# Attention and two mixtures of experts on one core: plain first layers accumulated in three PSUM banks, a fourth id table, lists ahead of weights

## The chip, the cores and the metric

The kernel runs on 1 core of a Trainium2 chip. The metric is the device time of one execution in microseconds (us); the number given for a kernel is the median of its runs. The kernel before takes 1922.17 us (three runs, 1922.14 to 1926.21).

## The reference

In float32: linear attention with exponential features over 4 batches, 8 heads, 576 positions and head size 64; its result, reshaped to 2304 tokens of 512 features, goes through a first mixture of 8 experts that uses every expert with weights balanced by 8 rounds of row and column scaling, and then through a second mixture that sends each token to one expert.

```python
# first mixture
P = np.exp(logits)
for _ in range(8):
    P /= P.sum(1, keepdims=True) + 1e-09
    P /= P.sum(0, keepdims=True) + 1e-09
    P *= N / E
for e in range(E):
    h = np.maximum(x @ w1[e], 0.0)      # 512 -> 1024
    out += P[:, e:e + 1] * (h @ w2[e])  # 1024 -> 512
# second mixture
logits = xn @ en.T / tau                # xn, en: normalised rows
expert_idx = np.argmax(logits, axis=1)
for e in range(E):
    h = np.maximum(x[mask] @ w1[e], 0.0)
    out[mask] = gate_w[mask, None] * (h @ w2[e])
```

## The kernel before

Every float32 operand is split in a high and a low part, so that one product of 128x128 by 128x384 is two contraction steps of three matmuls, six in all (`product`, L407, matmuls at L410 to L412).

The first mixture is cut in 16 groups n (8 experts, each with two halves of its hidden layer) and 3 blocks of 768 tokens. One group on one block is a half h, so h runs from 0 to 47; the program walks `HS` in that order. A two-by-two Strassen-like scheme replaces 8 products by 7. In groups 1 to 14 the second layer of one half is interleaved with the first layer of the next (`layers`, L465). Groups 0 (h = 0, 1, 2) and 15 (h = 45, 46, 47) are plain: `p1_group` (L564) makes the hidden layer in 14 products, seven for each j (a half of the hidden columns): A11, S2, S3, S1, A12, A22, S4, named by their weights; `p2_plain` then makes 16 products, which DVE adds to the accumulators at L833. h=0 is interleaved with the end of attention, since its generator `first` is created there and a piece is taken after each stage of the attention pipeline.

A finished quarter of the hidden layer goes through `put`: for n=0 `plain` (L417: ACT relu, then DVE's low part), for n=15 `gated`, where `gate` (L426) on DVE multiplies the relu with the token's weight into `graw` or in the bank; then ACT casts the high part (L432 or L442) and POOL (L443) or DVE (L433) subtracts for the low part. Each yield of a generator is a tick; a step is attached to tick k of half h by a table.

Routing for the second mixture: logits (`route_l`, `route_a`, L880), then small DVE work on the counts, which yields `meta` (offset, expert, and whether its weights have to be loaded, per block of 128 slots) and for each tile of 128 tokens the slots `si`. `route_i` (L951) on POOL scatters token number and gate of one tile into one of RB id tables in DRAM; a scatter that reuses a table waits for the earlier one on it. A block's list is the sum of the RB tables: `load_ids` (L1051, on SP) reads RB pieces at an offset taken from `meta` (`load_regs`), and `gather` (L1058 to L1064, on POOL) adds them, casts, and fetches the 128 rows by an indirect DMA. The tables are cleared at the start of the program.

`tail` is the table that places these steps in the last two halves: key k below 40 is tick k of h=46, from 40 on tick k-40 of h=47. Tiles 0 to 11 are routed there; the others (12 to 17) inside the first blocks of `second`.

`second` runs 22 blocks: `tx(i)` transposes the gathered rows on PE (L1103) and ACT and DVE split them (L1106, L1107); `p1(i)` is 24 matmuls (L1121 to L1123); `relu`; `th_`; `p2(i-1)` (L1154 to L1156). Weights come by `wcond` or `load_raws` (L1069, on SP) into raw buffers `rw`, and `wsplit` (L1094 ACT, L1095 DVE) makes the parts. `ob` yields the remaining routing of the other blocks in pieces, taken between splits. SP and POOL work their queues in the order written. The list of a block is wanted two blocks ahead; from NEARLY = 6 on, its rows can come from any tile.

## Time and profile before

| what | value |
|---|---|
| median of 3 runs | 1922.17 us (1922.14 to 1926.21) |
| the profiled execution | 1921.32 us |
| its span | 1919.1 us |
| mean granted clock of TensorE | 0.997 |
| busy: PE, DVE, ACT, POOL | 98%, 66%, 45%, 52% |
| chain that ended last: PE, POOL, issue, DVE, DMA, ACT | 69%, 13%, 8%, 4%, 3%, 2% |
| PE waiting for gathered rows (two transposes) | 5.9 us |

The profiled execution's own time holds 2.2 us outside the span. Busy times are sums over an engine's instructions; a row of a timeline gives start, length, the instruction with output and inputs, and in brackets the idle time before it with what ended it. The granted clock is a share of 2.4 GHz.

### The profile page before, as it was taken

Reading aid. Unit: us, or ns where it says so; the run is one execution under the profiler, and the core shown is the slowest. Engines: PE = TensorE matmul, PEld = TensorE weight load, DVE = VectorE, ACT = ScalarE, POOL = GpSimd, SP = SyncE. Lnnn points to the kernel's source line nnn. Section 1 sums busy time; section 2 is a strip of 40 time slices with the busy share of each in tenths; the row PEclk is TensorE's granted clock in tenths of the full one; section 3 lists DMA queues with packets and bytes.
Section 4 is the critical chain, followed back from the end, with each engine's and each line's share of the span. In section 5 each row is a group of like instructions: output and inputs, shape, how many; then the busy total and the mean of one; then the engine's idle time right before and its main releaser. Section 6 shows DMA issues by size and latency. Waiting matters only on the chain.

```text
span 1919.1 us, 34651 instructions
## 1 busy us (share of the span) xinstructions
PE 1881.9 (98%) x13636; PEld 1795.1 (94%) x13636; DVE 1272.0 (66%) x1610; ACT 861.4 (45%) x1258; POOL 995.8 (52%) x740
## 2 busy tenths in 40 slices
PE   9999999999999999999999999999999998999998
PEld 8899999999999999999999999999999987778886
DVE  6775565656657657566566565665665646899995
ACT  4674342433333333424243333333342333888885
POOL 0241377847466565747474666657483634542221
PEclk9999999999999999999999999999999999999999
DMA  5474634535372727354453637272645455162961
GB/s 162 141 275 174 233 130 172 168 131 191 109 229 97 255 77 240 108 191 145 154 176 124 212 103 248 82 250 93 209 128 171 133 169 132 51 222 87 331 213 35
DMA packets 121448, 314.28 MB, mean 164 GB/s; under 512 B 20136, under 2 KB 68408, under 8 KB 121282
## 3 DMA queue, kind: packets, MB, share of 16 engines
q1 hardware_dynamic: 117186, 301.51, 47.1%
q0 software_dynamic: 4096, 10.51, 1.8%
q8 instruction: 110, 1.80, 0.4%
q14 instruction: 56, 0.46, 0.1%
HBM read 335.27 MB, written 32.28 MB: 192 GB/s over the span
## 4 chain that ended last, share of the span: by engine, by line
PE 69%; POOL 13%; issue 8%; DVE 4%; DMA 3%; ACT 2%; SPq 0%; POOLq 0%; DVEq 0%; ACTq 0%
PE Q L411 16%; PE Q L412 15%; PE Q L410 15%; POOL w1S L330 2%; POOL hB L458 2%; POOL hT L458 2%; POOL w1A L330 2%; PE psR L144 2%; PE psD L201 2%; PE psA L1121 1%; PE psA L1122 1%; PE psA L1123 1%; PE psD L412 1%; PE psA L410 1%; PE psD L410 1%
## 5 line engine op out<-in xcount | busy, mean ns | idle before, releaser
L474 DVE TENSOR_TENSOR acca<-acca,Q 128x768 f32<-128x768 f32 x196 | 181.6, 950 | 143.6 <-PE Q L412 143.6
L410 PE MATMUL Q<-hT,w2S 128*128 128x384 f32 x504 | 169.4, 336 | 4.1 <-DVE rd L470 4.1
L458 POOL TENSOR_TENSOR hB<-rb,hB 128x768 fp32r<-128x768 f32 x42 | 77.6, 1846 | 181.7 <-ACT hB L455 181.7
L410 PE MATMUL Q<-xT,w1S 128*128 128x384 f32 x504 | 168.4, 334 | 0.9 <-ACT ra L479 0.9
L411 PE MATMUL Q<-hT,w2S 128*128 128x384 f32 x504 | 168.4, 334 | 0.0
L412 PE MATMUL Q<-hT,w2S 128*128 128x384 f32 x504 | 168.4, 334 | 0.0
L412 PE MATMUL Q<-xT,w1S 128*128 128x384 f32 x504 | 168.3, 334 | 0.0
L411 PE MATMUL Q<-xT,w1S 128*128 128x384 f32 x504 | 168.3, 334 | 0.0
L474 DVE TENSOR_TENSOR accb<-accb,Q 128x768 f32<-128x768 f32 x98 | 90.8, 950 | 73.3 <-PE Q L412 73.3
L470 DVE TENSOR_TENSOR Q<-Q,ra 128x768 f32<-128x768 f32 x42 | 40.6, 967 | 133.9 <-PE Q L412 133.9
L330 POOL TENSOR_TENSOR w1A<-raw,w1A 128x512 fp32r<-128x512 f32 x48 | 62.9, 1309 | 108.2 <-ACT w1A L329 108.2
L479 ACT COPY ra<-Q 128x768 f32<-128x768 f32 x42 | 33.6, 801 | 188.0 <-PE Q L412 166.8
L458 POOL TENSOR_TENSOR hT<-ra,hT 128x768 fp32r<-128x768 f32 x42 | 77.4, 1843 | 69.2 <-ACT hT L455 69.2
L412 PE MATMUL Q<-hB,w2A 128*128 128x384 f32 x336 | 112.3, 334 | 0.0
L412 PE MATMUL Q<-xB,w1A 128*128 128x384 f32 x336 | 112.2, 334 | 0.0
L410 PE MATMUL Q<-xB,w1A 128*128 128x384 f32 x336 | 112.2, 334 | 0.0
L411 PE MATMUL Q<-xB,w1A 128*128 128x384 f32 x336 | 112.2, 334 | 0.0
L410 PE MATMUL Q<-hB,w2A 128*128 128x384 f32 x336 | 112.2, 334 | 0.0
L411 PE MATMUL Q<-hB,w2A 128*128 128x384 f32 x336 | 112.2, 334 | 0.0
L1162 POOL DMA_INDIRECT out<-y,idt x22 | 27.5, 1248 | 158.4 <-ACT y L1161 97.5
L458 POOL TENSOR_TENSOR hT<-rd,hT 128x768 fp32r<-128x768 f32 x42 | 77.9, 1854 | 59.6 <-ACT hT L455 59.6
L1095 DVE TENSOR_TENSOR s1l<-rw,s1h 128x1024 fp32r<-128x1024 f32 x88 | 103.6, 1229 | 6.3 <-ACT s1h L1094 3.7
(432 smaller groups left out, 6150.6 us busy)
## 6 DMA issues: line engine op xcount, KB each, us to landing
xT<-xpd SPq DMA_DIRECT2D x120, 768.0 KB
rw<-in_moe_w SPq DMA_DIRECT2D x176, 512.0 KB
xB<-xpd SPq DMA_DIRECT2D x90, 768.0 KB
raw<-in_moe_w SPq DMA_DIRECT2D x34, 512.0 KB
gate<-gd SPq DMA_DIRECT2D x45, 384.0 KB
rx<-in_moe_w SPq DMA_DIRECT2D x30, 512.0 KB
xpd<-xT SPq DMA_DIRECT2D x12, 768.0 KB
xpd<-xB SPq DMA_DIRECT2D x9, 768.0 KB
```

What stands on the lines that cost most here:

```text
L144: T.matmul(hs[h_][:, c * P:(c + 1) * P], r[rs, c * P:(c + 1) * P], wphi[rs, :], start=True, stop=True)
L201: T.matmul(ps[cs, 2 * ci + h_, :], eq[:, sg, h_, ci * P + cs.start:ci * P + cs.stop], kvz[:, h_, sg, o:o + W], start=(sg == 0), stop=(sg = ...
L330: eng.tensor_tensor(out=t[:, 1], in0=r(nm), in1=f32(t[:, 0]), op=ALU.subtract)
L410: T.matmul(bank, w[:, 0, j, k, :], x[:, 0, k, :], start=start and k == 0, stop=False, skip_group_check=True)
L411: T.matmul(bank, w[:, 0, j, k, :], x[:, 1, k, :], start=False, stop=False, skip_group_check=True)
L412: T.matmul(bank, w[:, 1, j, k, :], x[:, 0, k, :], start=False, stop=stop and k == 1, skip_group_check=True)
L458: eng.tensor_tensor(out=hb[nm][:, 1], in0=src, in1=f32(hb[nm][:, 0]), op=ALU.subtract)
L470: V.tensor_tensor(out=out, in0=x, in1=y, op=op)
L474: V.tensor_tensor(out=z, in0=z, in1=ps, op=op)
L479: A.copy(m1c, b0)
L1095: V.tensor_tensor(out=lo, in0=r, in1=f32(hi), op=ALU.subtract)
L1162: G.indirect_dma_start(out=out, out_offset=bass.IndirectOffsetOnAxis(idt[i][:, :1], 0), in_=y, in_offset=None, bounds_check=NT - 1, oob_is ...
```

## The change

Four things, in one diff.

1. RB becomes 4: one more table is cleared, `load_ids` issues four reads, `gather` adds a 128x4 piece and then a 128x2 piece (two additions, as before), `route_i` uses table (t0+i) mod 4. The row sums of the balancing lie in a strided column of `pay`.
2. `p1_group` uses three banks per j in place of four. The new order is A11 in b0 (ACT copies it), A12 in b1 (DVE adds the copy, put), S2 on top of b0 (ACT copies), S3 in b2, S1 on top of b0 (ACT copies; DVE adds it to b2's into b1, put), then for j=0 the A11 of j=1 and for j=1 the first half product of `p2_plain` (not in h=0), A22 on top of b2 (DVE adds the copy, put), S4 on top of b0 (put). Per half DVE makes 6 adds instead of 10 and ACT 6 copies instead of 2. The products are the same.
3. In `tail` the lists of blocks 0 and 1 (tick 52) stand in front of all raw weights of the first layer (53; before, the weights stood at 49, 51 and 52 and the lists at 53 and 54). The splits `first_w1` move from 59-62 to 62-66, the gathers from 63 and 64 to 60.
4. In `second` five of the six scatters of tiles 12 to 17 come behind gather 4; the list of block 6 is loaded, and `ob` drained, before p1(3) instead of after its w2 splits; `ob`'s pieces are also taken during block 2.

```diff
-RB = 3
+RB = 4
...
-    def p1_group(n):
+    def p1_group(n, after=None):
...
+        def chain(j):
+            b0 = psum("A", [P, TH])
+            t = hp.tile([P, 2, TH], F32, tag="tu", name="tu")
+            live1[j] = b0, t
+            product(b0, 1, j, "A11", xs["B11"], True, True)
+            A.copy(t[:, 0], b0)
+
         for j in range(2):
-            b0 = psum("A", [P, TH])
-            product(b0, 1, j, "A11", xs["B11"], True, True)
-            tu, tv = (lambda t: (t[:, 0], t[:, 1]))(hp.tile([P, 2, TH], F32, tag="tu", name="tu"))
-            A.copy(tu, b0)
...
+            b0, t = live1[j]
+            product(b1, 1, j, "A12", xs["B21"], True, True)
+            add(b1, b1, t[:, 0])
+            put(0, 0, j, b1)
             yield
-            b1 = psum("A", [P, TH])
-            product(b1, 1, j, "S2", xs["T2"], True, True)
-            add(tu, b1, tu)
+            product(b0, 1, j, "S2", xs["T2"], False, True)
+            A.copy(t[:, 1], b0)
             yield
-            b2 = psum("A", [P, TH])
             product(b2, 1, j, "S3", xs["T3"], True, True)
-            add(tv, b2, tu)
             yield
-            b3 = psum("A", [P, TH])
-            product(b3, 1, j, "S1", xs["T1"], True, True)
-            add(b1, b3, tv)
+            product(b0, 1, j, "S1", xs["T1"], False, True)
+            A.copy(t[:, 0], b0)
+            add(b1, b2, t[:, 0])
             put(1, 1, j, b1)
             yield
-            product(b0, 1, j, "A12", xs["B21"], False, True)
-            put(0, 0, j, b0)
-            yield
+            if j == 0:
+                chain(1)
+                yield
+            elif after is not None:
+                next(after)
+                yield
             product(b2, 1, j, "A22", xs["T4"], False, True)
-            add(b2, b2, tu)
+            add(b2, b2, t[:, 1])
             put(1, 0, j, b2)
             yield
-            product(b3, 1, j, "S4", xs["B22"], False, True)
-            add(b3, b3, tu)
-            put(0, 1, j, b3)
+            product(b0, 1, j, "S4", xs["B22"], False, True)
+            put(0, 1, j, b0)
             yield
...
-        G.indirect_dma_start(out=ids[i % RB], out_offset=bass.IndirectOffsetOnAxis(si[:, i:i + 1], 0), in_=pay[:, t0 + i, :], in_offset=None)
+        G.indirect_dma_start(out=ids[(t0 + i) % RB], out_offset=bass.IndirectOffsetOnAxis(si[:, i:i + 1], 0), in_=pay[:, t0 + i, :], in_offset=None)
...
-    tail += [(49, partial(load_raws, 1, (0, 1))), (51, partial(load_raws, 1, (2,))), (52, partial(load_raws, 1, (3,)))]
-    tail += [(54, early_second), (54, start_second)] + [(53 + i, partial(load_ids, i)) for i in range(2)]
+    tail += [(52, partial(load_ids, 0)), (52, partial(load_ids, 1))]
+    tail += [(53, partial(load_raws, 1, range(4))), (54, early_second), (54, start_second)]
...
-            early = i + 3 > NEARLY
+            early = i + 3 >= NEARLY
+            if i + 3 == NEARLY:
+                for _ in ob:
+                    pass
             if early and i + 3 < i1:
                 load_ids(i + 3)
             p1(i)
```

How the queues change is shown at three places. The first is ACT's queue in h=45, in the products of j=1 (j=0's casts ahead of them); hB and hT are parts of the hidden layer, tu the copies, psA the banks. Before:

```order
817 L442 CAST hB_14643<-graw_14681 128x384
818 L442 CAST hB_14640<-graw_14681 128x384
819 L442 CAST hB_14642<-graw_14702 128x384
820 L442 CAST hT_14641<-graw_14702 128x384
821 L577 COPY tu<-psA_14716 128x384
822 L442 CAST hB_14643<-graw_14755 128x384
823 L432 CAST hB_14640<-psA_14716 128x384
824 L432 CAST hB_14642<-psA_14737 128x384
825 L442 CAST hT_14641<-graw_14755 128x384
826 L577 COPY tu<-psA_14914 128x384
```

and now:

```order
829 L441 CAST hB_14636<-grawwS_1_14661 128x384
830 L594 COPY tu<-psA_14642 128x384
831 L599 COPY tu<-psA_14642 128x384
832 L441 CAST hB_14639<-grawwS_1_14661 128x384
833 L579 COPY tu<-psA_14691 128x384
834 L441 CAST hB_14638<-grawwS_1_14707 128x384
835 L441 CAST hT_14637<-grawwS_1_14707 128x384
836 L432 CAST hB_14636<-psA_14722 128x384
837 L594 COPY tu<-psA_14691 128x384
838 L599 COPY tu<-psA_14691 128x384
839 L441 CAST hB_14639<-grawwS_1_14761 128x384
840 L432 CAST hB_14638<-psA_14723 128x384
```

Two copies (L594 of S2, L599 of S1) stand for each j where none stood, between the casts of gated quarters.

The second is SP's queue in h=47; rw are raw weights, idr the pieces of the lists, meta the offsets. Before:

```order
461 L1069 DMA rw_2_15744<-in_moe_w 128x1024
462 L1038 TENSOR_LOAD meta
463 L1038 ISA x2
464 L1039 TENSOR_LOAD meta
465 L1039 ISA x2
466 L1040 TENSOR_LOAD meta
467 L1040 ISA x2
468 L1069 ISA
469 L1069 DMA rw_3_15783<-in_moe_w 128x1024
470 L1051 ISA
471 L1051 DMA idr_15795<-ids_83 128x2
```

and now:

```order
461 L1053 TENSOR_LOAD meta
462 L1053 ISA x2
463 L1064 ISA
464 L1064 DMA idr_15765<-ids_83 128x2
...
477 L1064 ISA
478 L1064 DMA idr_15770<-ids_86 128x2
479 L1082 ISA
480 L1082 DMA rw_0_15785<-in_moe_w 128x1024
481 L1082 ISA
482 L1082 DMA rw_1_15787<-in_moe_w 128x1024
483 L1082 ISA
484 L1082 DMA rw_2_15789<-in_moe_w 128x1024
```

The pieces of both lists (eight reads, 464 to 478) are issued ahead of the first raw weight, where three loads and the fourth stood ahead of them.

The third is POOL's queue in the same half, with the scatters of tiles 6 to 11. Before:

```order
609 L443 TENSOR_TENSOR hB_15450<-graw_15631,hB_15450 128x384
610 L951 DMA ids_83<-pay,si_15590 19456x2
611 L443 TENSOR_TENSOR hT_15449<-graw_15631,hT_15449 128x384
612 L951 DMA ids_84<-pay,si_15590 19456x2
613 L951 DMA ids_85<-pay,si_15590 19456x2
614 L951 DMA ids_83<-pay,si_15590 19456x2
615 L951 DMA ids_84<-pay,si_15590 19456x2
616 L443 TENSOR_TENSOR hB_15451<-graw_15730,hB_15451 128x384
617 L951 DMA ids_85<-pay,si_15590 19456x2
618 L443 TENSOR_TENSOR hT_15449<-graw_15730,hT_15449 128x384
619 L1058 TENSOR_TENSOR ig_15939<-idr_15795 128x2
```

and now:

```order
609 L964 DMA ids_85<-pay,si_15580 19456x2
610 L442 TENSOR_TENSOR hB_15442<-grawwS_1_15637,hB_15442 128x384
611 L964 DMA ids_86<-pay,si_15580 19456x2
612 L442 TENSOR_TENSOR hT_15441<-grawwS_1_15637,hT_15441 128x384
613 L964 DMA ids_83<-pay,si_15580 19456x2
614 L964 DMA ids_84<-pay,si_15580 19456x2
615 L964 DMA ids_85<-pay,si_15580 19456x2
616 L964 DMA ids_86<-pay,si_15580 19456x2
617 L442 TENSOR_TENSOR hB_15443<-grawwS_1_15754,hB_15443 128x384
618 L442 TENSOR_TENSOR hT_15441<-grawwS_1_15754,hT_15441 128x384
619 L1071 TENSOR_TENSOR idr_15765<-idr_15765 128x4
```

Tables 83, 84, 85 took turns; now 85, 86, 83, 84 do, and the last scatter no longer stands behind a subtraction of h=47's last quarters.

## Rows read from the trace of the kernel before

**Rows 1.** The page: busy us of the engines, share of span, instructions.

```profile
PE 1881.9 (98%) x13636; PEld 1795.1 (94%) x13636; DVE 1272.0 (66%) x1610; ACT 861.4 (45%) x1258; POOL 995.8 (52%) x740
```

**Rows 2.** PE waits: line, tile, what ended them; us, times, longest.

```profile
PE psA L1103 <- DMA xgs<-x2d,idt: 5.9, 2, 3.3
```

**Rows 3.** PE waits from 1509 to 1626 us (h=45 to 47).

```profile
PE psA L410 <- DVE graw L426: 2.1, 2, 1.4
...
PE psA L410 <- DVE tu L566: 1.1, 1, 1.1
PE psD L410 <- ACT hB L432: 0.7, 2, 0.4
...
PE psD L411 <- DVE hB L433: 0.2, 1, 0.2
```

**Rows 4.** Timeline of PE, h=2: start, length, instruction, [idle before, releaser].

```profile
247.25 0.45 PE L410 MATMUL psA<-xT,w1A 128*128 128x384 f32 x1 [0.57 <-DVE tu L566]
```

**Rows 5.** PE by line, h=45: busy, mean ns, then idle before.

```profile
L411 PE MATMUL psD<-hB,w2A 128*128 128x384 f32 x24 | 8.1, 339 | 0.1
```

**Rows 6.** Timelines of PE (h=47, then h=46) and ACT.

```profile
1596.78 0.44 PE L410 MATMUL psA<-xT,w1S 128*128 128x384 f32 x1 [1.44 <-DVE graw L426]
1597.06 0.34 PE L411 MATMUL psA<-xT,w1S 128*128 128x384 f32 x1
...
1539.69 0.33 PE L412 MATMUL psA<-xB,w1A 128*128 128x384 f32 x1
...
1540.06 0.48 ACT L577 COPY tu<-psA 128x384 f32<-128x384 f32 x1 [14.70 <-PE psA L412]
```

**Rows 7.** Timeline of PE at tx(0) and tx(6).

```profile
1628.46 0.86 PE L1103 MATMUL psA<-ident,xgs 128*128 128x128 f32 x4 [2.61 <-DMA xgs<-x2d,idt]
...
1702.37 0.63 PE L1103 MATMUL psA<-ident,xgs 128*128 128x128 f32 x4 [3.31 <-DMA xgs<-x2d,idt]
```

**Rows 8.** Windows: PE, PEld, DVE, ACT, POOL busy (x), clock, DMA share, GB/s.

```profile
1590.00:1600.00 10.00, 7.93 (x44) 7.25 (x44) 9.28 (x32) 2.68 (x6) 7.73 (x7) 1.00 0.04 16
1630.00:1634.00 4.00, 4.00 (x9) 2.88 (x10) 3.69 (x4) 4.00 (x5) 1.89 (x3) 0.50 0.09 13
1634.00:1638.40 4.40, 4.40 (x17) 3.28 (x15) 4.40 (x5) 3.11 (x4) 3.98 (x5) 0.82 0.26 62
...
1680.00:1690.00 10.00, 10.00 (x51) 8.34 (x50) 9.96 (x13) 9.23 (x13) 5.08 (x2) 1.00 0.19 54
```

**Rows 9.** Timeline of DVE, h=45 and h=47.

```profile
1518.83 0.57 DVE L566 TENSOR_TENSOR psA<-psA,tu 128x384 f32<-128x384 f32 x1 [0.48 <-PE psA L412]
...
1599.56 1.09 DVE L1006 CAST meta<-ebx 1x6 int32<-1x6 f32 x1
```

**Rows 10.** Timeline of SP: first start, length, count.

```profile
1602.20 4.22 SPq L1069 DMA_DIRECT2D rw<-in_moe_w  x4
1615.48 3.60 SPq L1051 DMA_DIRECT2D idr<-ids  x6
1619.37 4.11 SPq L1069 DMA_DIRECT2D rw<-in_moe_w  x8
...
1687.80 4.32 SPq L1051 DMA_DIRECT2D idr<-ids  x5
```

**Rows 11.** Timeline of POOL: last scatter and first gather.

```profile
1611.75 0.98 POOL L951 DMA_INDIRECT ids<-pay,si  x1 [3.27 <-DMA ids<-pay,si]
...
1620.91 1.01 POOL L1064 DMA_INDIRECT xgs<-x2d,idt  x1 [0.69 <-DMA idr<-ids]
```

**Rows 12.** Timeline of ACT: casts of raw weights.

```profile
1610.17 1.05 ACT L1094 CAST s1h<-rw 128x1024 fp32r<-128x1024 f32 x1 [1.18 <-DMA rw<-in_moe_w]
...
1616.48 2.00 ACT L1094 CAST s1h<-rw 128x1024 fp32r<-128x1024 f32 x2 [2.22 <-DMA rw<-in_moe_w]
...
1623.06 1.05 ACT L1094 CAST s2h<-rw 128x1024 fp32r<-128x1024 f32 x1 [1.30 <-DMA rw<-in_moe_w]
```

**Rows 13.** Timeline of POOL: the gather of block 6.

```profile
1696.59 1.00 POOL L1064 DMA_INDIRECT xgs<-x2d,idt  x1 [0.28 <-POOL idt L1062]
```

More of the change, by code (lines that the diff above doesn't have):

```diff
@@ L273, in misc_comp @@
         V.tensor_copy(iob, itmp3)
[L274 removed]
+        V.tensor_copy(pay[:, :, 0], tokid[:, 0:NTL])
         V.memset(half, 0.5)
@@ L434, in gated @@
             return
-        if hv == 1 and th == 1:
-            raws["g"] = wp.tile([P, 1024], F32, tag=("wS1_1", "wS4_1")[j], name=f"graw{j}")
-        elif hv == 1:
-            raws["g"] = wp.tile([P, 1024], F32, tag="wS2_1", name="graw2")
+        place = {(0, 0, 0): "wS1_1", (1, 0, 0): "wS2_1", (1, 1, 1): "wS4_1"}.get((hv, th, j))
+        if place:
+            raws["g"] = wp.tile([P, 1024], F32, tag=place, name="graw" + place)
         k = (hv, th) in ((0, 0), (0, 1))
@@ L775, in sinkhorn @@
         A.activation(out=Pp, in_=Pm, func=AF.Exp)
-        rs = c0.tile([P, NTL], F32, name="rs")
+        rs = pay[:, :, 1]
         cs = c0.tile([P, E], F32, name="cs")
+        c0.tile([P, 24], F32, name="cpad")
         for it in range(8):
@@ L1057, in gather @@
         r = idr.pop(i)
+        G.tensor_tensor(out=r[:, 0:2, :], in0=r[:, 0:2, :], in1=r[:, 2:4, :], op=ALU.add)
         G.tensor_tensor(out=ig, in0=r[:, 0, :], in1=r[:, 1, :], op=ALU.add)
-        G.tensor_tensor(out=ig, in0=ig, in1=r[:, 2, :], op=ALU.add)
         gt[i] = ig[:, 1:2]
@@ L1286, in build @@
     tail += route_steps(6, (24, 26, 28, 40, 40, 41), (24, 25, 26, 40, 41, 41), p=41, b=41, o=41, c=42, d=43, s=44, w=45, i=(45, 46, 47, 48, 49, 50))
-    tail += [(k, partial(next, rf, None)) for k in (43, 44, 46, 47, 49)] + [(48, partial(load_regs, 0)), (52, partial(load_regs, 1))]
-    tail += [(49, partial(load_raws, 1, (0, 1))), (51, partial(load_raws, 1, (2,))), (52, partial(load_raws, 1, (3,)))]
-    tail += [(54, early_second), (54, start_second)] + [(53 + i, partial(load_ids, i)) for i in range(2)]
+    tail += [(k, partial(next, rf, None)) for k in (43, 44, 46, 47, 49)] + [(48, partial(load_regs, 0)), (49, partial(load_regs, 1))]
+    tail += [(52, partial(load_ids, 0)), (52, partial(load_ids, 1))]
+    tail += [(53, partial(load_raws, 1, range(4))), (54, early_second), (54, start_second)]
     tail += [(55, partial(load_raws, 2, range(4)))]
-    tail += [(59 + c, partial(first_w1, 0, (c,))) for c in range(4)]
+    tail += [(k, partial(first_w1, 0, (c,))) for c, k in enumerate((62, 64, 65, 66))]
     for i in range(3):
@@ L1294, in build @@
     tail += [(66, partial(first_w2, 0, (0,)))]
-    tail += [(63, partial(gather, 0)), (64, partial(gather, 1)), (66, partial(load_ids, 2)), (67, partial(load_ids, 3))]
+    tail += [(60, partial(gather, 0)), (60, partial(gather, 1)), (66, partial(load_ids, 2)), (67, partial(load_ids, 3))]
     tail += [(69, partial(tx, 0))]
@@ L1326, in build @@
         else:
-            gen, tick = (p1_group(n), 0) if h else (first, filled[0])
-            for part in (gen, p2_plain(n, bi)):
+            second_ = p2_plain(n, bi)
+            gen, tick = (p1_group(n, second_), 0) if h else (first, filled[0])
+            for part in (gen, second_):
                 for _ in part:
@@ L1398, in second @@
             relu(1)
-            for k in range(NTL - NA):
-                route_i(t0, k)
+            route_i(t0, 0)
             first_w1(2, (2,))
@@ L1404, in second @@
             gather(4)
+            for k in range(1, NTL - NA):
+                route_i(t0, k)
             first_w1(2, (3,))
@@ L1420, in second @@
             if i + 1 < i1:
-                w1_next(i, range(4), partial(next, ob, None) if i > 2 else no)
+                w1_next(i, range(4), partial(next, ob, None))
             relu(i)
@@ L1425, in second @@
             w2_this(i, partial(next, ob, None))
-            if i + 3 == NEARLY:
-                for _ in ob:
-                    pass
-                load_ids(i + 3)
             if i > i0:
```

16 lines of the change are left out of this document (11 added, 5 removed).

## The prediction

> **What bounds the kernel now.** I read the page first: PE is busy 1881.9 of 1919.1 us [rows 1], so only the 37 us in which PE does nothing, or runs at a lower clock, can be won, and every new PE wait is lost one for one. The second view is the list of PE's waits: its largest entry is not arithmetic, but two transposes that wait for gathered tokens, 5.9 us together [rows 2]. The same list cut to the last three plain halves (h = 45, 46, 47) shows 2.1 us on results of the gate and 1.1 on DVE's adds, all in h=47, 0.7 on ACT's casts in two pieces and 0.2 on a subtraction [rows 3]; in h=2 one product waits 0.57 for an add [rows 4], and h=45 shows 0.1 [rows 5]. Each gap costs about 0.27 more than it shows: a modelled end lies 0.33 after its start while the next matmul normally starts 0.17 after (0.16), and a restart takes 0.28 instead of 0.17 (0.11) [rows 6]. So h=2 loses 0.85 and a little more (I count 1.1), h=45 0.4, h=46 (one of the casts and the subtraction) about 1.0, and h=47, with four such gaps and smaller ones, about 5.1. The two gather stalls are read from the timeline of PE: tx(0) 2.61, tx(6) 3.31 [rows 7], so 2.8 and 3.5 lost. Behind the first the granted clock falls to 0.50, PE's lower level of 1.2 GHz [rows 8].
>
> **Part 1, plain first layers.** The products stay: 30 of six matmuls per half, 1.05 us each at 0.174. Per half DVE loses four adds and ACT gains four copies, so DVE becomes freer; the question is what PE now waits for. In the old order A22 too continued in a bank that DVE reads, but S3's, two products further back. Now it continues in the bank from which DVE has just added S1's sum: last matmul of S1 at s, ACT's copy from s+0.37 for 0.48, DVE's add from about s+0.9 for 0.56, PE again at about s+1.5 [rows 6, 9]. With one product between (the next A11, or a half product of p2) PE would want to go on at s+1.22: 0.27 plus 0.11 of restart, 0.38 lost, twice a half. Without one it goes on at s+0.17, and 1.43 is lost.
> - h=0 has no p2 to borrow from (its generator is built without it): j=1 pays 1.43; j=0 runs among attention's products and I charge nothing. +1.4.
> - h=1: 0.76 at most; the balancing of the gate (Sinkhorn) puts its own small products between some of these, so I take +0.45. h=2: 0.76 and some 0.15 for p2's last half product behind S4, against 1.1 now: -0.2.
> - h=45 (gated): 0.76; S1 waits for ACT's copy of S2, which stands in ACT's queue behind a cast that waits for DVE's gate, about 0.45 in each j; p2's last half product stands directly behind S4 and waits for a cast on ACT and a subtraction on DVE, 0.95. Sum 2.6 against 0.4: +2.2.
> - h=46: the same, but routing's transposes run between the products, and 1.0 is lost already: +0.4.
> - h=47: the queues in order cost most here. DVE is full with routing (9.28 of 10 us, [rows 8]), and a cast of six numbers takes 1.09 there [rows 9]; the copy for S1 stands behind a cast behind a gate behind that chain, and I count 3 to 3.7 for this wait, 1 for S3, 0.95 for p2: 5.85 against 5.1. +0.75.
>
> Sum of part 1: +5.0. Bounds: 0, if each copy hides as the two copies per half of today mostly do, and +8, if h=46 pays what h=45 does and h=47 two us more. I take 5.0, worked out from durations of the same instructions.
>
> The Trainium skill (Perfetto Trace Analysis, section Matmuls) says that independent matmul groups should rotate through different PSUM banks so that the evacuation of one overlaps the next. By that rule taken whole, all 24 added copies would be exposed; this is the last rival below.
>
> **Part 2, lists first, four tables.** Now SP issues four raw weight loads from 1602.20 to 1606.4, then waits, issues six list reads at 1615.48, and more weights at 1619.37 [rows 10]. The reads wait for the scatters: the last is issued at 1611.75, after 3.27 of waiting for the one three back [rows 11]; nothing of the weights hides that, and the transfer beside them lands about 3.6 later. With four tables a scatter waits for the fourth back, and with the weights behind the lists the two no longer share the DMA engines. Counted from the start of h=47 (1580.6 now), the scatters come about 7 us earlier (DVE has four adds less in their way), all land by +30 instead of +34.8, and eight list reads of 0.6 take 4.8 instead of 3.6. Gather 0 is issued at about +34 instead of +40.3 [rows 11], and with its slowest landing of today, 7.5, it is there by +41.5; PE wants it at +45.2. The stall at tx(0) goes: -2.8. The extra issue of two reads per block (1.1 us of SP) lies beside PE and is charged at nothing; its cover is SP's idle time.
>
> With the stall gone the clock does not fall. p1(0) has 24 matmuls of 0.23, 5.6; at 0.50 and 0.82 it took 8.4 [rows 8]: 2.8 to win. But ACT and DVE work off the weight splits meanwhile, DVE being busy 9.96 of 10 later [rows 8], so I give 0.9 back: -1.9. Bounds -2.8 and 0.
>
> The price: the first raw weights are issued at about +32.5 instead of +21.6. Today the first cast comes 8.0 after the first issue and the last two from 14.3 on, beside scatters; the first of the next four, in an emptier stretch, 3.7 (issue 1619.37, cast 1623.06) [rows 10, 12]. After 3.7, and 1.4 for each further, all four are there by +41 and cost nothing; at today's slow pace the last is cast at about +47, and its split ends some 5 us after p1(0) could begin. I take the row of the second four, since no scatter is left then, and +0.5. Bounds 0 and +5.3.
>
> The Trainium skill (DMA: Bandwidth & Descriptors, section Latency and other measured facts) gives HBM latency as 0.2 us on average and 2 us at high load. With 2 us on each of four loads the last would be late by about 2, and the sum 1.5 higher.
>
> **Part 3, the list of block 6 before p1(3).** Now it is read at 1687.80 behind a row of weights; POOL's adds and cast stand behind the scatter of an earlier block's output, and the gather goes out at 1696.59 [rows 10, 13] and lands at 1702.3. Moved ahead by one block (12.3 us of PE) it is there by about 1694: -3.5. The price is that the rest of block routing is drained before p1(3), in a stretch where DVE is full; what is late next is the split of the weights for block 4, and I charge 0 since each hook still follows one split. Bounds 0 and +3 (half of the routing's DVE time of that stretch). Moving scatters behind gather 4 costs POOL's queue nothing before block 6.
>
> **Sum**: 5.0 - 2.8 - 1.9 + 0.5 - 3.5 = -2.7, against the profiled 1921.3; that run stands 0.85 below the median of 1922.17. On the median the forecast is **1919.5**.
>
> **The rivals.**
> 1. The plain halves hide their copies. For it: DVE is relieved, and the gaps of h=47 come from DVE. Against: queue order on ACT. Part 1 falls to 0 or below: 1922.2 - 7.7 = 1914.5.
> 2. Slower: the first weights behind the lists. If all four land at the pace of the first four now (decided where the last lands later than +43), p1(0) begins 5.3 late instead of 0.5, and PE idles long enough that the clock falls as it did behind tx(0): -2.7 + 4.8 + 1.9 = +4.0, and with block 1's weights a further us late, 1927. For it: the slow landings are in the trace. Against: they ran beside scatters.
> 3. It does not do what it says: tx(6)'s stall goes, but DVE, at 9.96 of 10, makes a split late instead, and 3.5 is given back: 1923.
> 4. The bank rule: 24 copies each exposed by 0.85 - 0.17 = 0.68, 16.3 instead of 5.0: 1930.8. Against: a product stands between most copies and the next use. This is what the rule of the Trainium skill's Perfetto Trace Analysis, section Matmuls, would do here.
>
> **How the numbers follow.** A measurement can tell 0.2%, 3.84 us, from no change: faster is below 1918.3, slower above 1926.0. Forecast 0.44 (faster 0.19, same 0.25), rival 1 0.19 (faster), rival 2 0.20 (same 0.06, slower 0.14), rival 3 0.12 (same 0.09, slower 0.03), rival 4 0.05 (slower). Faster 0.38, same 0.40, slower 0.22. The range runs from rival 1's 1914.5 to rival 2's 1927; rival 4 and the tails are left out.
>
> **What would show it.** Part 1: gaps before A22 in h=45 near 0.1 shown, one of 1.2 in h=0, one of 3 in h=47. Part 2: no wait for xgs at tx(0), granted clock 1.00 throughout, first cast of a raw weight 3.7 after its issue. Part 3: PE's wait for xgs gone from the list, and no wait for s1l in its place. A clock below 1.00 in h=47 or p1(0), or casts at 8 after issue, would make the prediction wrong.

## The result, and the profile after

The changed kernel takes 1939.97 us (median of 4 runs, 1938.84 to 1941.22) against 1924.05 for the kernel before in the same comparison: the ratio is 1.0086, 95% interval 1.0073 to 1.0098, about 16 us slower. The prediction said 1919.5 with a range to 1927, so the time lies outside it, and on the other side. The profiled executions are 1941.22 (span 1939.4) and 1921.32 (span 1919.1), 20.3 apart by span: the sum below is made for these two and is some 4 us more than the medians show.

The page's busy times answer to [rows 1]: PE is busy 4.4 us longer with the same 13636 matmuls, a lower clock among it; the rest is waiting.

```profile
PE 1886.3 (97%) x13636; PEld 1797.6 (93%) x13636; DVE 1262.5 (65%) x1586; ACT 871.4 (45%) x1282; POOL 995.1 (51%) x740
```

PE's waits answer to [rows 2, 3] (engine, tile, line, what ended them: us, times, longest). L1116 is what L1103 was, L594 the copy of S2, L579 the copy of A11, L565 DVE's adds, L846 its accumulator adds, L1134 p1.

```profile
PE psA L1116 <- DMA xgs<-x2d,idt: 11.5, 1, 11.5
PE psA L410 <- ACT tu L594: 6.3, 4, 3.7
...
PE psA L1134 <- ACT xth L1119: 2.3, 1, 2.3
...
PE psA L410 <- DVE psA L565: 2.2, 6, 1.2
PE psA L410 <- ACT tu L579: 2.0, 1, 2.0
...
PE psB L925 <- DVE oh L917: 1.2, 1, 1.2
PE psD L410 <- DVE accb L846: 0.9, 1, 0.9
```

Two waits on gathered rows were there before, 5.9 us; one is left, and it is 11.5, at another block. The waits on ACT's copies are new.

How late the same piece of work starts after the change, from the first matmul of each stretch in the two traces:

| piece | before | after | later by |
|---|---|---|---|
| h=0 | 149.70 | 149.96 | 0.3 |
| h=1 | 192.64 | 194.41 | 1.8 |
| h=2 | 233.03 | 235.45 | 2.4 |
| after h=2 | 266.94 | 270.98 | 4.0 |
| h=45 | 1507.19 | 1511.19 | 4.0 |
| h=46 | 1538.82 | 1545.11 | 6.3 |
| h=47 | 1580.62 | 1588.05 | 7.4 |
| last matmul of h=47 | 1625.51 | 1636.93 | 11.4 |
| p1(0) | 1630.00 | 1639.98 | 10.0 |
| transposes of block 5 | 1686.61 | 1707.90 | 21.3 |
| transposes of block 6 | 1702.37 | 1722.71 | 20.3 |

So 11.2 us are lost in the plain halves and the end of h=47, 1.4 come back up to p1(0), 11.3 are lost between p1(0) and block 5, and 1.0 comes back at block 6. After block 6 nothing changes.

The second large loss is the one that the prediction did not have at all. First PE's wait, then POOL's timeline up to it (start, length, instruction, idle before and its releaser), then DVE's:

```profile
1707.90 1.09 PE L1116 MATMUL psA<-ident,xgs 128*128 128x128 f32 x4 [11.50 <-DMA xgs<-x2d,idt]
```

```profile
1678.09 3.06 POOL L1175 DMA_INDIRECT out<-y,idt  x1 [0.30 <-issue]
1686.50 4.13 POOL L1175 DMA_INDIRECT out<-y,idt  x1 [5.35 <-ACT s L1107]
1690.64 4.32 POOL L1071 TENSOR_TENSOR idr<-idr 128x4 f32<-128x4 f32 x1
1695.04 0.19 POOL L1072 TENSOR_TENSOR ig<-idr 128x2 f32<-128x2 f32 x1
...
1696.15 5.38 POOL L1077 DMA_INDIRECT xgs<-x2d,idt  x1 [0.66 <-PE psA L1136]
```

```profile
1684.56 0.67 DVE L1153 TENSOR_TENSOR hTl<-psA,hTh 128x512 fp32r<-128x512 f32 x1
1685.16 4.61 DVE L1108 TENSOR_TENSOR s1l<-rw,s1h 128x1024 fp32r<-128x1024 f32 x4
1689.69 0.67 DVE L1120 TENSOR_TENSOR xtl<-psA,xth 128x512 fp32r<-128x512 f32 x1
1690.30 1.20 DVE L1108 TENSOR_TENSOR s<-rw,s 128x1024 fp32r<-128x1024 f32 x1
1691.43 3.47 DVE L1108 TENSOR_TENSOR s2l<-rw,s2h 128x1024 fp32r<-128x1024 f32 x3
1694.83 0.67 DVE L1153 TENSOR_TENSOR hTl<-psD,hTh 128x512 fp32r<-128x512 f32 x1
...
1696.03 4.61 DVE L1108 TENSOR_TENSOR s1l<-rw,s1h 128x1024 fp32r<-128x1024 f32 x4
```

Read the two side by side. An addition of 128x4 numbers takes POOL 4.32 us, until 1694.96; DVE's run of weight splits, which began at 1690.30, ends at 1694.90. While DVE reads PSUM (hTl), POOL's next addition takes 0.19. Then DVE starts the next run at 1696.03, POOL issues the gather at 1696.15, and the issue takes 5.38. In this stretch POOL stands while DVE subtracts one SBUF operand from another, back to back, and moves in the openings between. The two outputs ahead of gather 5 (p2's results are written one after the other, so the second waits for the first to land) push it past one opening, and each opening missed costs 4 to 5 us.

The issue ends at 1701.53, 5.1 us into PE's wait; the other 6.4 pass until the rows land. In these 6.4 the DMA engines are full with raw weights (the last two numbers are the DMA share and GB/s):

```profile
1701.50:1707.90 6.40, 0.00 (x0) 0.03 (x1) 0.00 (x0) 0.00 (x0) 2.62 (x6) 0.50 0.99 359
```

In lists_late (below) the same issue takes 5.38 too, and the rows land 2.6 us after its end, at a DMA share of 0.69; the wait is 7.7. So a late gather also meets the next weights; no run tests this part alone.

Not every run of these subtractions holds POOL. A later run of four in the same trace lets it in whenever one of them ends. The lines are POOL's cast and issue for gather 7, DVE's run beside them, and ACT's four casts for that run; the last line is ACT's casts for the run that began at 1696.03:

```profile
1720.56 1.06 POOL L1075 CAST idt<-ig 128x1 int32<-128x1 f32 x1
1721.90 1.70 POOL L1077 DMA_INDIRECT xgs<-x2d,idt  x1 [0.27 <-POOL idt L1075]
1719.22 4.63 DVE L1108 TENSOR_TENSOR s1l<-rw,s1h 128x1024 fp32r<-128x1024 f32 x4
1718.11 3.91 ACT L1107 CAST s1h<-rw 128x1024 fp32r<-128x1024 f32 x4
1691.65 3.91 ACT L1107 CAST s1h<-rw 128x1024 fp32r<-128x1024 f32 x4
```

The run at 1719.22 starts on the heels of ACT's first cast. The one at 1696.03 starts when all four casts are done: DVE had fallen behind. All traces but no_low's show this split from 1626 us on: of the POOL instructions that begin inside such a run, before its last subtraction, none of 346 was held to the run's end where the run's first subtraction follows its cast within 0.12 us, and 75 of 88 were held where the cast had been done longer. No run here changes that alone, so that DVE's lag is the cause is not shown.

The Trainium skill (SBUF — State Buffer, section SBUF: two separate sides) says that DVE and GpSimd share a port pair under an exclusive lock, held for the whole instruction, also for a DVE instruction with two SBUF inputs against a GpSimd one that reads SBUF. The trace agrees on who stands: 4.13 to 5.38 beside the runs of blocks 3 to 5, 0.2 to 1.0 in the openings. On how long it agrees for the run at 1719.22 only: in the others POOL stands for three or four instructions of 1.2 us in a row.

The third place is the start of the second mixture. SP, ACT and DVE (its rows answer to [rows 10, 12]):

```profile
1612.60 12.53 SPq L1064 DMA_DIRECT2D idr<-ids  x8
1625.51 10.40 SPq L1082 DMA_DIRECT2D rw<-in_moe_w  x11
```

```profile
1629.01 1.05 ACT L1107 CAST s1h<-rw 128x1024 fp32r<-128x1024 f32 x1 [10.15 <-DMA rw<-in_moe_w]
```

```profile
1630.09 1.22 DVE L1108 TENSOR_TENSOR s1l<-rw,s1h 128x1024 fp32r<-128x1024 f32 x1 [4.70 <-ACT s1h L1107]
1631.23 0.55 DVE L846 TENSOR_TENSOR accb<-psD,accb 128x384 f32<-128x384 f32 x1
```

```profile
SPq L1064 <- DMA ids<-pay,si: 8.5, 3, 5.0
```

SP's eight reads take 12.5 us, 8.5 of it in three waits for scatters to land (the last line); the first raw weight is issued behind them, at +37.5 (us from h=47's start). DVE's queue waits 4.70 for it, with an accumulator add behind it for which PE waits.

The windows show PE's clock (PE, PEld, DVE, ACT, POOL busy, clock, DMA share, GB/s), to be held against [rows 8]:

```profile
1610.80:1614.20 3.40, 3.40 (x12) 3.40 (x12) 1.27 (x4) 0.48 (x1) 1.91 (x2) 0.50 0.02 1
1640.00:1648.20 8.20, 7.61 (x34) 5.63 (x38) 8.20 (x9) 7.15 (x8) 2.82 (x4) 0.79 0.16 37
1696.40:1707.90 11.50, 0.00 (x1) 0.03 (x1) 4.24 (x4) 0.62 (x2) 7.72 (x6) 0.64 0.67 222
1707.90:1718.00 10.10, 10.10 (x40) 8.38 (x41) 5.54 (x6) 5.79 (x8) 0.00 (x0) 0.74 0.09 36
```

The granted clock falls to 0.50 in h=47, where it stayed at 1.00 in the kernel before: PE had just waited 3.67 for the copy of S2, and ten of the next twelve matmuls follow at 0.32 in place of 0.174. It still falls in p1(0), after PE's 2.3 us wait for xth, and again behind the wait of 11.5: 0.74 over 10.1 us takes back 2.6 of what the removed stall at block 6 gives.

### The profile page after: what moved, and what is told of

Same layout as the page of the kernel before. It is cut to its first block, busy times and chain, and to the rows that moved or that the text cites. A ratio compares the mean times of both kernels' runs of the same rounds, so it can differ in the third digit from the quotient of the medians.

```text
span 1939.4 us, 34724 instructions
## 1 busy us (share of the span) xinstructions
PE 1886.3 (97%) x13636; PEld 1797.6 (93%) x13636; DVE 1262.5 (65%) x1586; ACT 871.4 (45%) x1282; POOL 995.1 (51%) x740
## 4 chain that ended last, share of the span: by engine, by line
PE 69%; POOL 14%; issue 7%; DVE 4%; DMA 3%; ACT 3%; SPq 0%; POOLq 0%; DVEq 0%; ACTq 0%
PE Q L411 15%; PE Q L412 15%; PE Q L410 15%; POOL w1S L330 3%; POOL hB L457 2%; POOL hT L457 2%; POOL w1A L330 2%; PE psA L1135 2%; PE psA L1136 2%; PE psA L1134 2%; PE psD L201 2%; PE psR L144 1%; PE psD L1167 1%; PE psD L1169 1%; PE psD L1168 1%
```

## The experiments

The kernel before had its own runs beside each group of four (medians 1924.56, 1925.53, 1924.15, and 1919.15 for the last two), so kernels are compared by their ratio to it. In some kernels the runs fall into two groups with 8 to 11 us between them; then both are given. A profile is of one run of a kernel.

**The new plain layers alone** (plain_alone): the kernel before with `p1_group` of the change, its ticks in XFREE (when an operand's buffer is given free) and its places for the gate's results graw.

```diff
-    def p1_group(n):
+    def p1_group(n, after=None):
...
-            gen, tick = (p1_group(n), 0) if h else (first, filled[0])
+            second_ = p2_plain(n, bi)
+            gen, tick = (p1_group(n, second_), 0) if h else (first, filled[0])
```

> The kernel before with the new plain first layers alone. Theory A (PE waits for ACT's copies and DVE's adds in queue order, wherever the plain form stands): the three first halves lose about 3.8 us and the three last about 7 as in the changed kernel, h=47 3 to 4 of them; both gather stalls stay, 2 to 3.3 each; 1930 to 1934. Rival B (h=47's loss comes from the moved steps of the tail, not from the form): h=47 loses under 1.5, 1927 to 1929.

1930.72 us, ratio 1.0036 (1.0024 to 1.0048). At the end of h=47 it is 9.3 us later than before, 3.7 by the end of h=2 and 3.2 in h=47. Its waits:

```profile
PE psA L1115 <- DMA xgs<-x2d,idt: 5.0, 2, 2.9
PE psA L410 <- ACT tu L594: 4.8, 4, 2.1
```

Theory A: the form itself costs this, without any of the tail's moves. Both gather stalls are still there. In h=47 the granted clock falls to 0.50 here too, twice for 3.4 us.

**The change without the plain layers** (no_plain): the diff above, the other way round, on the changed kernel.

> The changed kernel with the old plain first layers: lists first, four tables, scatters behind gather 4 and the early list stay. Theory A (the wait of 11.5 us before the transposes of block 5 comes from POOL: scatters in front of it and its instructions standing while DVE splits weights back to back): that wait stays at 5 to 12 us, the wait at block 0 is gone, 1923 to 1929. Rival B (it comes from the whole start being 10 us late beside the same weights): the wait is under 2 us, 1914 to 1918.

1932.7 us, ratio 1.0043 (1.0031 to 1.0055). With the 0.36% of plain_alone that makes 0.79% of the 0.86%.

```profile
PE psA L1104 <- DMA xgs<-x2d,idt: 11.3, 1, 11.3
PE psD L410 <- DVE accb L834: 4.2, 1, 4.2
```

The wait at block 5 does not hang on the late start (p1(0) begins at 1630.00, as before), so rival B falls; the kernel is a little slower than A allowed, for a wait that neither named: 4.2 us on DVE's accumulator adds.

**All scatters ahead of gather 4 again** (scatters_first):

```diff
-            route_i(t0, 0)
+            for k in range(NTL - NA):
+                route_i(t0, k)
...
-            for k in range(1, NTL - NA):
-                route_i(t0, k)
```

> The changed kernel with all six scatters of the last tiles in front of gather 4 again. Theory A (the five scatters behind gather 4 push the output scatters and gather 5 into the stretch in which DVE never stops): the wait before block 5 falls from 11.5 to under 4 us, 1928 to 1934. Rival B (the routing drained early takes DVE and so POOL, whatever the order of the scatters): it stays at 8 to 12, 1937 to 1941.

Five runs at 1926.92 to 1929.42 and five at 1940.34 to 1942.99; ratio 1.0056 (1.0032 to 1.0081) over both. The profile is of the first group, 1927.84, and its wait at block 5 is 1.9. A for half of the runs; that the other half stays where B has it was nobody's expectation. The profiles of this kernel and of splits_later (below) show how near the two lie. Here output 1 is issued at 1683.46, in the opening of the two hTl; POOL, then DVE:

```profile
1683.46 0.99 POOL L1175 DMA_INDIRECT out<-y,idt  x1 [3.66 <-ACT hr L1144]
1684.45 4.01 POOL L1071 TENSOR_TENSOR idr<-idr 128x4 f32<-128x4 f32 x1
...
1689.62 4.81 POOL L1077 DMA_INDIRECT xgs<-x2d,idt  x1 [0.64 <-PE psA L1149]
```

```profile
1683.19 0.67 DVE L1153 TENSOR_TENSOR hTl<-psA,hTh 128x512 fp32r<-128x512 f32 x1
1683.79 4.61 DVE L1108 TENSOR_TENSOR s1l<-rw,s1h 128x1024 fp32r<-128x1024 f32 x4
```

**First splits later** (splits_later): the changed kernel with the old plain layers and all scatters ahead of gather 4 (no_plain_scatters_first, below), and

```diff
-    tail += [(k, partial(first_w1, 0, (c,))) for c, k in enumerate((62, 64, 65, 66))]
+    tail += [(k, partial(first_w1, 0, (c,))) for c, k in enumerate((66, 67, 68, 69))]
```

> The changed kernel with the old plain layers, all scatters ahead of gather 4, and the first splits of raw weights four to three ticks later (66 to 69). Theory A (PE's wait of 4.65 in h=47 comes from DVE's queue: accumulator adds behind a split whose raw weights have not landed): the wait falls under 2, while p1(0) starts no more than 1.5 us earlier, for its weights are still the last to come. Rival B (the adds themselves or their banks): it stays over 4.

One run, 1937.9. The accumulator wait is gone, as A has it, but PE then waits 8.5 for xth, whose cast stands behind those same splits on ACT: the late weights are paid in one queue or the other, and p1(0) begins at 1635.57, against 1631.04 without the edit. And at block 5 PE waits 10.9, although the scatters stand in front. Output 1 comes at 1682.22, 0.06 after the run has begun:

```profile
1682.22 5.42 POOL L1163 DMA_INDIRECT out<-y,idt  x1 [4.06 <-ACT xth L1107]
1687.64 4.34 POOL L1059 TENSOR_TENSOR idr<-idr 128x4 f32<-128x4 f32 x1
...
1693.13 5.40 POOL L1065 DMA_INDIRECT xgs<-x2d,idt  x1 [0.64 <-PE psA L1124]
```

```profile
1682.16 4.61 DVE L1096 TENSOR_TENSOR s1l<-rw,s1h 128x1024 fp32r<-128x1024 f32 x4
```

One opening missed, three instructions at 4.3 to 5.4. By these two profiles, of two kernels, whether gather 5 is in time hangs on a few tenths of a microsecond at output 1; no run moves output 1 alone.

**No subtraction for four sets of weights** (no_low): no_plain, with the low parts of two sets of each layer's weights set to zero.

```diff
-        V.tensor_tensor(out=lo, in0=r, in1=f32(hi), op=ALU.subtract)
+        if (which, i) in ((1, 4), (1, 5), (2, 3), (2, 4)):
+            V.memset(f32(lo), 0.0)
+        else:
+            V.tensor_tensor(out=lo, in0=r, in1=f32(hi), op=ALU.subtract)
```

> The changed kernel with the old plain layers, in which the low parts of four sets of split weights (first layer of blocks 4 and 5, second layer of blocks 3 and 4) are set to zero in place of being subtracted, so that these products are less exact. Theory A (POOL stands while DVE subtracts two SBUF operands back to back): POOL's adds and issues between outputs 1 and gather 5 take 0.2 to 1.1 us each in place of 4 to 5.4, and the wait of 11.3 at block 5 falls under 3. Rival B (the scatters' and gathers' own transfers are slow): the wait stays over 7.

One run, 1919.06, 10 us under the lowest of no_plain's ten (1929.14); no wait at block 5. POOL, with the scatters still behind gather 4 and the drain still early:

```profile
1679.43 0.98 POOL L1166 DMA_INDIRECT out<-y,idt  x1 [6.16 <-ACT s2h L1095]
1680.42 0.22 POOL L1059 TENSOR_TENSOR idr<-idr 128x4 f32<-128x4 f32 x1
...
1681.83 1.00 POOL L1065 DMA_INDIRECT xgs<-x2d,idt  x1 [0.66 <-POOL idt L1063]
```

Theory A. DVE is still busy, with fills of 0.91 that read nothing, 0.16 apart; POOL's instructions go at their own length beside them. The issue that took 5.38 in no_plain takes 1.00.

**The routing and the list of block 6 late** (lists_late), in the changed kernel:

```diff
-            early = i + 3 >= NEARLY
-            if i + 3 == NEARLY:
-                for _ in ob:
-                    pass
+            early = i + 3 > NEARLY
...
-                w1_next(i, range(4), partial(next, ob, None))
+                w1_next(i, range(4), partial(next, ob, None) if i > 2 else no)
...
+            if i + 3 == NEARLY:
+                for _ in ob:
+                    pass
+                load_ids(i + 3)
```

> The changed kernel with the routing of the other blocks and the list of block 6 as late as before. Theory A (scatters behind gather 4 are the cause, and small DVE work of the routing leaves POOL its openings): gather 5 goes out while routing's small instructions run, the wait before block 5 is under 4 us, but one of 3 to 8 returns before block 6; 1931 to 1937. Rival B (the early drain alone is the cause): no wait before block 5 and 3.3 before block 6, 1930 to 1932; the two overlap in time and are told apart by the waits.

1930.79 to 1937.94, ratio 1.0047 (1.0031 to 1.0063). The profile is the longest run: a wait of 7.7 at block 5 and none at block 6. The scatters behind gather 4 are enough for a wait there, against B; against A, it is not under 4, and the list of block 6 comes in time.

**Gathers half a block earlier** (hoisted), in the changed kernel:

```diff
             if i + 1 < i1:
                 tx(i + 1)
+            if i + 3 < i1 and i + 3 in idr:
+                gather(i + 3)
```

> The changed kernel, scatters still behind gather 4 and lists in front, with the gathers from block 5 on written half a block earlier, ahead of output scatter 1. Theory A (gather 5 is late because it stands in POOL's queue behind output 1, which waits for output 0, which stands behind the scatters): the wait before block 5 falls from 11.5 to under 4, 1928 to 1933. Rival B (the gather's own instructions are what DVE holds up, wherever they stand): 8 to 11.5 stays, 1937 to 1941.

1933.92 (four runs, 1930.64 to 1934.57), ratio 1.0055 (1.004 to 1.007), just above A's range. In the profile, of the fastest, the wait at block 5 is gone, with 0.5 at block 6 and 4.3 at block 7: A for block 5, and a later gather meets a later run.

**The cast behind the copy** (put_later): plain_alone, with

```diff
             add(b1, b1, t[:, 0])
-            put(0, 0, j, b1)
             yield
...
             A.copy(t[:, 1], b0)
+            put(0, 0, j, b1)
             yield
```

> The kernel before with the new plain layers, in which the cast of the first finished quarter is written behind ACT's copy of S2, not ahead of it. Theory A (S1 waits because ACT's copy of S2 stands in ACT's queue behind a cast that waits for DVE): the wait of 2.1 us in h=47 and the three of about 0.5 to 1 on that copy fall by half or more, 3 to 4 us less than with the form of the change. Rival B (DVE's backlog itself is the limit): the waits only move to later products, under 1 us less.

Ratio 1.0014 (1.0004 to 1.0023) against 1.0036. No wait on L594 is left, and before p2's last products the plain halves cost 6.4 in place of 9.6; 1.5 come back as a wait on the accumulators.

```profile
PE psA L410 <- DVE psA L565: 3.8, 6, 1.4
...
PE psA L410 <- ACT tu L579: 1.9, 1, 1.9
...
PE psD L410 <- DVE accb L845: 1.5, 1, 1.5
```

So the order of ACT's queue makes 3 of the 9 us, going by the two profiles; the adds before A22 and the copy of A11 are the largest waits left.

**Tables, lists and drain apart, with the old plain layers.** no_plain_scatters_first joins two edits above: lists in front, early list, scatters ahead of gather 4.

> The changed kernel with the old plain layers and all scatters ahead of gather 4; the lists stay in front of the weights. Theory A: no wait over 2 us at block 5; PE waits 3 to 5 us in h=47 for DVE's accumulator adds, which stand in DVE's queue behind the split of raw weights that land late; within 3 us of before. Rival B (the accumulator wait has to do with the scatters): that wait is under 1 us and the kernel 4 to 8 us faster than before.

Ratio 1.0002 (0.9985 to 1.0019); eight runs to 1924.91, two at 1933.05 and 1934.73. The wait at block 5 is 1.9 in the profile, that on the accumulators 4.65. Against no_plain (1.0043) the place of the scatters is worth 0.4%.

weights_first has the tail of before, four tables and the early list; against no_plain_scatters_first:

```diff
-    tail += [(k, partial(next, rf, None)) for k in (43, 44, 46, 47, 49)] + [(48, partial(load_regs, 0)), (49, partial(load_regs, 1))]
+    tail += [(k, partial(next, rf, None)) for k in (43, 44, 46, 47, 49)] + [(48, partial(load_regs, 0)), (52, partial(load_regs, 1))]
-    tail += [(52, partial(load_ids, 0)), (52, partial(load_ids, 1))]
-    tail += [(53, partial(load_raws, 1, range(4))), (54, early_second), (54, start_second)]
+    tail += [(49, partial(load_raws, 1, (0, 1))), (51, partial(load_raws, 1, (2,))), (52, partial(load_raws, 1, (3,)))]
+    tail += [(54, early_second), (54, start_second)] + [(53 + i, partial(load_ids, i)) for i in range(2)]
...
-    tail += [(k, partial(first_w1, 0, (c,))) for c, k in enumerate((62, 64, 65, 66))]
+    tail += [(59 + c, partial(first_w1, 0, (c,))) for c in range(4)]
...
-    tail += [(60, partial(gather, 0)), (60, partial(gather, 1)), (66, partial(load_ids, 2)), (67, partial(load_ids, 3))]
+    tail += [(63, partial(gather, 0)), (64, partial(gather, 1)), (66, partial(load_ids, 2)), (67, partial(load_ids, 3))]
```

> The kernel before with four tables and the early list of block 6 alone: old plain layers, raw weights ahead of the lists, all scatters ahead of gather 4. Theory A (the fourth table and the early list help, the lists in front and the moved scatters cost): the accumulators of h=47 don't wait, the wait at block 0 falls from 2.6 to under 1, the one at block 6 goes and none over 2 us comes at block 5; 4 to 8 us faster than before. Rival B (early draining of the routing is what starves POOL): a wait of 5 to 11 at block 5, slower than before by 2 to 8.

Ratio 0.9997 (0.9979 to 1.0015): eight runs at 1918.40 to 1922.40, four at 1931.89 to 1932.84. By their time a third of the runs are slow in B's way, or worse, but the profile is of a run of the first group: its wait at block 5 is 1.9, and the one at block 6 is gone. A's gain of 4 to 8 did not come. Block 0 still waits 1.2, behind a wait of 2.1 on the accumulators: the fourth table did not bring the gathers forward (gather 0 goes out at 1621.10; before, at 1620.91). SP's eight reads run from 1609.07 to 1618.81, although the last scatter is issued at 1604.91.

early_list_alone is the early drain and list on the kernel before, three tables:

```diff
-            early = i + 3 > NEARLY
+            early = i + 3 >= NEARLY
+            if i + 3 == NEARLY:
+                for _ in ob:
+                    pass
...
-                w1_next(i, range(4), partial(next, ob, None) if i > 2 else no)
+                w1_next(i, range(4), partial(next, ob, None))
...
-            if i + 3 == NEARLY:
-                for _ in ob:
-                    pass
-                load_ids(i + 3)
```

> The kernel before with the early list of block 6 and the early drain of routing alone (three tables, scatters ahead of gather 4). Theory A: the wait at block 6 goes, gather 5 is late in some runs only: 1918 to 1922 in most, 1930 to 1933 in the others. Rival B (the early list needs the fourth table): the wait at block 6 stays over 2 and the time is within 2 us of before.

Ratio 1.0019 (1.0000 to 1.0037), runs from 1920.17 to 1937.84, three of ten at 1930 or more. The wait at block 6 is gone in the profile and 1.8 stands at block 5: A, with worse runs than it had (two of the ten within its 1918 to 1922).

list_mid drains half a block later than that (the diff is against the kernel before):

```diff
+            if i + 3 == NEARLY:
+                for _ in ob:
+                    pass
+                load_ids(i + 3)
             w2_this(i, partial(next, ob, None))
-            if i + 3 == NEARLY:
-                for _ in ob:
-                    pass
-                load_ids(i + 3)
```

> The kernel before, in which the rest of the routing is drained and the list of block 6 read after the transposes of block 4, ahead of block 3's second splits, not behind them (half a block earlier than before, half a block later than in the change). Theory A (POOL's chain to gather 5 needs the openings that routing's small DVE instructions leave, and the early drain spends them too soon): no wait over 2 us at block 5, the wait of 3.3 at block 6 falls under 1.5, no run of the longer mode; 2 to 4 us faster than before. Rival B (whatever brings the list forward takes POOL from gather 5): a wait of 4 or more at block 5 in some runs.

Ratio 0.9997 (0.9988 to 1.0006), all eleven runs within 1916.54 to 1922.59. No run of the longer kind, as A has it; but no gain: in the profile a wait of 3.6 at block 7 has taken the place of the 3.3 at block 6.

lists_first_alone adds four tables and the lists in front to that:

> The same with four tables and the lists ahead of the raw weights as in the change; old plain layers, scatters ahead of gather 4. Theory A (the lists in front cost about 4 us on the accumulators of h=47 and give back the stall of 2.8 at block 0; the scatters land one after the other whatever the number of tables): within 2 us of list_mid, and no longer mode. Rival B (the fourth table brings the gathers forward): 3 to 6 us faster than list_mid.

Ratio 1.0001 (0.9990 to 1.0011), 1914.91 to 1924.12. The wait at block 0 is gone, one of 2.9 on the accumulators has come, 1.8 is left at block 6: within noise of list_mid, as A had it. It differs from no_plain_scatters_first only in when the routing is drained and the list of block 6 read, as list_mid does from early_list_alone: with the later drain none of 22 runs lies more than 0.3% above the kernel before, with the early one five of 20 do.

**A version put together from the parts** (best): weights_first with the gathers of hoisted and

```diff
-    tail += [(59 + c, partial(first_w1, 0, (c,))) for c in range(4)]
+    tail += [(k, partial(first_w1, 0, (c,))) for c, k in enumerate((62, 64, 65, 66))]
```

> The kernel before with four tables, the early list of block 6, every gather from block 5 on written directly behind the transposes that free its buffer (half a block earlier, ahead of the output scatter), and the first splits at ticks 62 to 66. Theory A: gather 5 is out of reach of DVE's long runs, so none of the runs shows the mode that is 11 us longer; no wait of PE over 1.5 us at blocks 5 or 6 and none over 1 on the accumulators; 5 to 8 us faster than before in every run. Rival B (the longer mode has another cause than gather 5): a third of the runs stay near 1932.

Ratio 0.9991 (0.9978 to 1.0005), 1916.58 to 1928.84. No run at 1932, as A has it, and no gain, against A: the profiled run has waits of 5.7 at block 0 and 4.9 at block 7. No version that was run is shown to beat the kernel before.

## Why the prediction was wrong

**Part 1, +5.0 with a bound of +8: measured 11.2, and 9.3 alone.** The mechanism was right and the size was off, and one term was missing. By halves, forecast and measured: h=0 +1.4 and 1.5; h=1 +0.45 and 0.7; h=45 +2.2 and 2.3; these hold. The steps that failed: "h=2 ... -0.2" (1.6: PE waits 1.99 there for the copy of S2, which stands on ACT behind a relu and a weight cast; I had billed that wait only to the gated halves); "h=46 ... +0.4" (1.1: PE waits 0.46 there for the copy of S2; the rest is not taken apart); and "h=47 ... 5.85 against 5.1: +0.75". In h=47 the wait for S1 came as forecast, 3.67 against "3 to 3.7". It is the chain of queues that I had worked out: DVE's small routing work, its gate, ACT's cast, then the copy.

```profile
1609.65 0.48 ACT L432 CAST hB<-psA 128x384 fp32r<-128x384 f32 x1 [3.81 <-DVE psA L426]
1610.03 0.49 ACT L594 COPY tu<-psA 128x384 f32<-128x384 f32 x1
```

But the other waits of h=47 add to it: 1.96 for the copy of A11, 1.25 for routing on DVE, and 0.93 for the accumulators, which part 2 brings. And the clock was put at nothing: behind the wait of 3.67 it stands at 0.50 for 3.4 us, which costs about 1.5 (ten steps between matmuls at 0.32 in place of 0.174). "A clock below 1.00 in h=47" was a sign of being wrong, and it came. The loss from h=47's start to its last matmul grew by 4.0, 3.2 of it in plain_alone. The sum for h=47 was off in itself, too: 3 to 3.7, 1 and 0.95 make 4.95 to 5.65, not 5.85. Put_later shows by how much the order of ACT's queue makes the loss. The rule on PSUM banks from the Trainium skill (Perfetto Trace Analysis, section Matmuls) pointed the right way; its full price of 16.3 was not reached, since a product does stand between most copies and the next use.

**Part 2: -2.8, -1.9 and +0.5: measured -1.4 beside a late PE, and nothing alone (p1(0) begins at 1630.00 in no_plain too).** "All land by +30" failed. The scatters were issued early as forecast (the last at 1612.30, +24.3), but the landings were the bound, not the issues: the reads that wait for the fourth and the fifth start at 1618.23 and 1620.90, 8.5 and 9.9 after their scatters were issued, the sixth has landed by 1621.47 (+33.4), and SP is done at +37. Such landings stood in the trace of before. The third scatter of the row, issued at 1602.07, took 9.4 there, and the wait of 3.27 in [rows 11] is for it; the fourth, issued at 1604.89, held SP's first read until 1615.48. The forecast's +34.8 ("about 3.6 later") is the time of that read; the last scatter landed 5.4 after its issue, at +36.5. With the fourth table the wait on POOL went; it moved to SP. So gather 0 left at +38.1, not +34. The stall at tx(0) did go, with some luck: PE comes to it at +49, not at +45.2, and whether the rows would have been there at +45.2 is not shown. The term "+0.5" failed by its place rather than its row: the first cast does come 3.5 after its issue (3.7 forecast), but the issue is at +37.5, not +32.5, and what waits is not p1(0) alone. DVE's queue stands at the first split, and p2's accumulator adds behind it; I had costed the weights' lateness and not named what is queued behind the waiting instruction. That is 4.2 in no_plain, and splits_later shows the same lateness in ACT's queue. "The clock does not fall" failed with it: it fell after PE's wait for xth, and p1(0) took 8.2 against 8.4.

**Part 3: -3.5: measured +11.3 up to block 5, less about 1 at block 6.** The list of block 6 did come in time, and the stall there went; the low clock behind the new wait took most of that back. The step that failed is "moving scatters behind gather 4 costs POOL's queue nothing before block 6", with "what is late next is the split of the weights for block 4". Late next was gather 5. Rows 8 had DVE at 9.96 of 10, and I read it as a limit on DVE alone; that POOL stands for it could be read from two rows of before, the issue of 4.07 at 1654.04 and, in front of block 6, a cast of 128 numbers that takes 4.79:

```profile
1691.52 4.79 POOL L1062 CAST idt<-ig 128x1 int32<-128x1 f32 x1
```

I had put the delay of gather 6 down to its late list and the output in front of it.

Rival 3 had the right place (DVE full between blocks 3 and 6) and the wrong victim. The runs show that the long wait at block 5 needs DVE's subtractions (no_low), that with the moved scatters and the early drain together every run is long (no_plain, 1929.14 at the lowest), and that the early drain without them makes some runs long (early_list_alone, weights_first, no_plain_scatters_first; none in list_mid and lists_first_alone). No run of these longer groups was profiled, so that they too wait at block 5 is inferred from their time and from splits_later. What decides it from run to run was not caught in two profiles of one kernel; the tenths at output 1 are read from two kernels.

## What to carry to other kernels

When a step is moved on an engine, look at what another engine does in the stretch that it moves into: a queue that is on no critical path lost 4 to 5 us per instruction here beside runs of two-operand DVE work that had fallen behind. A wait in a queue in order is paid by what stands behind it, so price late data by the instruction behind the one that reads it. A wait for a buffer that is removed gains little where the transfers land late all the same: read the landing first. And price a new PE wait with the clock that falls behind it.

## What was not expected of the hardware

POOL additions of 128x4 and the issue of an indirect DMA take 4.0 to 5.4 us where they begin early in a DVE run of four subtractions of two SBUF operands whose data had long been ready, and 0.2 to 1.0 beside reads of PSUM or fills; they end with the run to within 0.1 us, or 0.9 after it, an issue's own length. Beside runs that follow ACT's casts directly none took more than 2.1. Of a row of six scatters of one tile each, some landed 4.1 to 5.4 us after their issue and others 8.5 to 10.6, in the kernel before as in the change; what sets it is not shown. And a kernel's runs can fall into two groups about 10 us apart, by the traces for a margin of some tenths at one instruction.
